# Linear attention and gated MLP in one kernel: the head's inverse roots on GpSimd, its normalizations on ScalarE

## Chip, cores and metric

The kernel runs on one core of one Trainium2 chip. The metric is the time of one execution on the device, in microseconds (us). The engines are TensorE (PE in the profile, PEld for its weight loads), VectorE (DVE), ScalarE (ACT), GpSimd (POOL) and SyncE (SP), which issues the DMAs.

## The reference

Two parts follow each other: attention without a softmax, with 64 product features, and a gated MLP whose gate mixes along the sequence. Batch 4, 4 heads, 1088 positions, head size 32, so d_model is 128; d_ff is 1024.

```python
phi(x) = outer(S1 @ x, S2 @ x)                     # 8 x 8 features
attn   = (phi(q) @ (phi(k)^T v)) / (phi(q) @ sum(phi(k)) + 1e-6)
h      = gelu_tanh(attn @ w_in)
u, v   = h[:512], h[512:]
v_n    = (v - mean(v)) / sqrt(var(v) + 1e-6) * g_ln
v_s    = w_sg @ v_n + b_sg                         # along the 1088 positions
out    = attn + (u * v_s) @ w_out
```

## The kernel before

The sequence is cut into nine tiles of 128 positions (the last one holds 64 real ones) and, where it is the moving axis, into three chunks of about 363. Products that need full precision take each operand as a high and a low part (fp32r) and three matmuls; the low part is the difference of the value and its rounded high part, one DVE subtraction each.

The **head** does batch 0 up to its first spatial product, while the weights come in. Its steps: `k1`, `kp`, `k2`, `kv` build the attention's sums; `q2`, `qa`, `qp` the features of q; `q3`, `xt`, `tr`, `x1`, `x2` the attention's output, transposed into a high part `x_h` (ACT) and a low part `x_l` (DVE), three tiles at a time; `v1` the gate half of h for one tile of positions (three matmuls into `pv`); `gelu` on ACT; `bn` its statistics on DVE (`mv`). Then, for three groups of three tiles (`GROUPS`), `v2` computes the inverse root of the variance of three tiles at once, in 12 DVE instructions of three elements per partition (a start value by integer shift, then two steps of Newton's kind), which end in `rs`, the inverse root, and `nm`, minus mean times `rs`. `v3` normalizes one tile of v in place: on ACT for the tiles in `VA` (4, 6 and 8), on DVE for the others. `z` is the spatial product of one tile with one chunk, as a plain fp32 product of two matmul records (27 of them). Beside this stand the splits of `w_in` in two halves (`wi1`, `wi0`, seven 512-element DVE steps and two for the low part each) and of `w_out` (`wo`), the high parts of w (`whi`, ACT) and its low parts (`wlo`, DVE, 1.3 us each). A low part `w_l[t]` is needed by the main loop and may start when tile t-1 has had its products.

The head's order isn't written out. Each step is given to `Steps.at` with its engine, its assumed length, what it comes after, the PSUM banks that it takes, an extra delay (`late`), and a `tail`. `Steps.order` then goes through the head as a list planner: it takes the step that can start first, unless one on the same engine that becomes ready before that step's end has a way to the end that is longer by 0.5; among equals the longer way goes first. Loads go in their given order on SP, each with an assumed time to landing of 2 us plus what its place in the bytes so far (`self.dma`, in KB) gives at an assumed rate. The engines then run their instructions in this order; a step that is planned before its input really lands makes its engine wait, with all that is queued behind.

The **main loop** does, per batch, the spatial product of the other three column blocks (and of all four for later batches), the gate, and the output product, with the next batch's attention and statistics spread between (`Side`, with due times in `FIRST` and `LATER`). Its instructions are ordered by the framework's scheduler, not by `Steps`. Its first matmuls are queued behind the head's last `z`.

Of the kernel before, what the change touches and what calls it, by code (L numbers as in the profile page):

```python
# [11 lines left out]
I32 = mybir.dt.int32  # L12
I64 = mybir.dt.int64
AF = mybir.ActivationFunctionType
ALU = mybir.AluOpType
# [3 lines left out]
P = 128  # L19
NT = 9  # L20
SP = NT * P
# [6 lines left out]
EPS = 1e-6  # L28
# [1 line left out]
EX = (2, 4, 7)  # L30
FL = 7
GROUPS = ((0, 3), (3, 3), (6, 3))
VA = (4, 6, 8)
WARM = 14


# [18 lines left out]
def f32(ap):  # L55
    return ap.bitcast(F32)
# [11 lines left out]
def tile_kernel(ctx: ExitStack, tc: tile.TileContext, qd, kd, vd, sd, wd, bd, wind, gd, woutd, identd, outd):  # L68
    nc = tc.nc
    mm = nc.tensor.matmul  # L70
    V, A, G = nc.vector, nc.scalar, nc.gpsimd
# [11 lines left out]
    def run(steps):  # L83
        for _ in steps or ():
            pass
# [38 lines left out]
    class Attention:  # L124
# [4 lines left out]
        def load_kv(self):  # L129
            self.k = self.pool([P, SP], "kld", f"k{self.b}")  # L130
            load(self.k, kd[self.b])
            for p in range(2):
                load(vx[:, p * (NT + 1) : p * (NT + 1) + NT], vd[self.b, :, p])
# [42 lines left out]
        def load_q(self, j):  # L176
            ci, p = divmod(j, 2)
            c0, cw = CH[ci]
            self.q[j] = q = self.pool([P, CW], "qld", f"q{self.b}_{j}")
            for r in range(2):  # L180
                load(q[64 * r : 64 * r + 64, :cw], qd[self.b, 64 * p : 64 * p + 64, c0 : c0 + cw])
# [262 lines left out]
    class Plan:  # L444
# [5 lines left out]
        def at(self, times, f, *args, name=None, after=()):  # L450

            if not isinstance(times, tuple):
                todo = [lambda: f(*args)]
                times = (times,)
            else:
                state = {}

                def step(i):
                    if i == 0:
                        state["g"] = f(*args)  # L460
                    if i + 1 < len(times):
                        next(state["g"])
                    else:
                        run(state["g"])

                todo = [lambda i=i: step(i) for i in range(len(times))]
            n = len(self.steps)
            for i, t in enumerate(times):
                if n + i < len(self.over):
                    t = self.over[n + i]  # L470
                self.steps.append([t, todo[i], [n + i - 1] if i else after])
            if name is not None:
                self.names[name] = n, len(times)
# [96 lines left out]
    class Head:  # L570
# [7 lines left out]

        def load(self, name, kb, f, after=(), queue="SP"):
            self.dma += kb  # L580
            self.s.at(name, queue, 0.47 if queue == "SP" else 0.1, f, after, late=2.0 + max(0.0, self.dma / 260 - 1.5))

        def split64(self, name, hi, lo, raw, n, whole, after, late):

            tl = {}

            def tile(x):
                if x not in tl:
                    tl[x] = self.stage([P, n], f"d{x}" if n > 16 else f"s{x}", name + x, F32 if x in "te" else I32)
                return tl[x]  # L590

            def word(i):
                return raw().bitcast(I32).rearrange("p (n two) -> p n two", two=2)[:, :, i]

            d = 0.08 + n / 950
            t, e, g, m = (lambda x=x: tile(x) for x in "tegm")
            ti, ei = lambda: t().bitcast(I32), lambda: e().bitcast(I32)
            ops = [

                lambda: V.tensor_scalar(ti(), word(1), 3, 0x3FFFFFFF, op0=ALU.logical_shift_left, op1=ALU.bitwise_and),  # L600
                lambda: V.scalar_tensor_tensor(ti(), word(1), -(1 << 30), ti(), op0=ALU.bitwise_and, op1=ALU.bitwise_or),

                lambda: V.tensor_scalar(m(), word(1), 0x7FFFFFFF, None, op0=ALU.bitwise_and),
                lambda: V.scalar_tensor_tensor(t(), m(), float(0x38100000), t(), op0=ALU.is_ge, op1=ALU.mult),

                lambda: V.tensor_scalar(ei(), word(0), 8, None, op0=ALU.logical_shift_right),
                lambda: V.tensor_scalar(g(), ti(), -(1 << 23), None, op0=ALU.bitwise_and),
                lambda: V.scalar_tensor_tensor(e(), ei(), 2.0**-44, f32(g()), op0=ALU.mult, op1=ALU.mult),
            ]
            last = after  # L610
            for i, f in enumerate(ops):
                self.s.at((name, i), "V", d, f, last, late=0.07)
                last = [(name, i)]
            if whole is not None:
                self.s.at((name, "whole"), "V", d, lambda: V.tensor_add(whole, t(), e()), last, late=0.07)
            more = [(name, "whole")] if whole is not None else []
            self.s.at((name, "hi"), "A", 0.1 + n / 1000, lambda: A.copy(hi, t()), [(name, 3)], late=0.08, tail=late)
            self.s.at(
                (name, "l1"), "V", d, lambda: V.tensor_sub(t(), t(), f32(hi)), [(name, "hi"), (name, 5)] + more, late=0.07
            )  # L620
            self.s.at((name, "l2"), "V", d, lambda: V.tensor_add(lo, t(), e()), [(name, "l1"), (name, 6)], late=0.07, tail=late)

        def build(self):
            at, pool, stage, g = self.s.at, self.pool, self.stage, self.g
# [130 lines left out]
            for c in range(3):  # L755
                at(("k1", c), "PE", 0.8, lambda c=c: k1(c), ["sk", "k0" if c == 0 else "k1"], [(("pk", c), "ps", 3)])
                at(("kb", c), "A", 0.2, lambda c=c: copy_b(c), [("k1", c)], late=0.1)
                for i in range(3):
                    t = 3 * c + i
# [21 lines left out]
            for j in range(6):  # L781
                c, p = divmod(j, 2)
# [7 lines left out]
            n = 2 * (D + 1)  # L790
            pd, px, den, xt = {}, {}, {}, {}
# [75 lines left out]
                at(("gelu", t), "A", 0.52, lambda t=t: gelu(t), [("v1", t)], (), [("pv", t)], late=0.1)  # L867
                at(("bn", t), "V", 0.8, lambda t=t: stats(t), [("gelu", t)], late=0.05)
            for t0, n_ in GROUPS:
                gen = g.v2(t0, n_)  # L870
                at(("v2", t0), "V", 1.8, lambda gen=gen: run(gen), [("bn", t) for t in range(t0, t0 + n_)], late=0.06)
                last = [("v2", t0)]
                for t in range(t0, t0 + n_):
                    if t in VA:
                        at(("v3", t), "A", 0.72, lambda t=t: g.v3(t), last, late=0.1)
                    else:
                        at(("v3", t), "V", 0.35, lambda t=t: V.tensor_scalar(  # L877
                            g.vn[:, t], g.vn[:, t], g.mv[:, t, 0:1], g.rs[:, t : t + 1], op0=ALU.subtract, op1=ALU.mult
                        ), last, late=0.08)
            zs = self.zs = []  # L880

            def z(t, ci):
# [26 lines left out]
            for i in range(3):  # L909
                gen = g.split(1, 3 * i, 3)  # L910
# [6 lines left out]
    def xtiles(b, xp):  # L917
        return [xp.tile([P, SP], F32R, name=f"x{b % 2}_{i}", tag=f"x{b % 2}_{i}") for i in "hl"]
# [3 lines left out]
    side = Pool(sp, 1, r=8, kp=3, kb=2, qld=1, qt=3, st=2, vh=2, vl=2, ve=3, y=3, h=3, p=3)  # L922

    x0 = xtiles(0, xp0)
    g = Gate(0, side, x0)
    with tc.tile_pool(name="stage", bufs=1) as stp:
        head = Head(side, Pool(stp, 1, wst=2, kb0=2, den=2, bst=2), x0, g)
        head.build()
        head.last = head.s.run(("z", NT - 1, 2), ("vl", 2), ("whi", NT - 1))
        zs = head.zs  # L930
    xp1 = ctx.enter_context(tc.tile_pool(name="x1", bufs=1, reuse_waits="tile"))
    gp = ctx.enter_context(tc.tile_pool(name="gate", bufs=2, reuse_waits="tile"))
    late = Pool(gp, 3, gt=4)
    pend = []

    def start():

        gts = [g.scale(late, zs[ci], 0, ci) for ci in range(3)]

        def unit(ci):  # L940
            pend.append(g.gate(late, gts[ci], g.unit(late, 0, ci), 0, ci))

        return [lambda ci=ci: unit(ci) for ci in range(3)] + 2 * [lambda: flush(late, *pend.pop(0))]
# [42 lines left out]
    for b in range(B):  # L986
        first, extra = (1, start()) if b == 0 else (0, [])
        if b + 1 < B:
# [7 lines left out]
            g = s.g  # L996
# [40 lines left out]
```

## Time and profile before

| | |
|---|---|
| median of three runs | 372.48 us (372.02 to 372.65) |
| the profiled execution | 372.73 us, span 370.9 us |
| PE busy | 356.7 us (96%) |
| DVE busy | 267.2 us (72%) |
| ACT busy | 160.0 us (43%) |
| POOL busy | 23.5 us (6%) |
| mean granted PE clock | 0.987 of 2.4 GHz |

The span reaches from the first to the last instruction; the device time also holds what lies around it. A busy share is a mean over stages that have different limits, so the stages are read one by one. In a row of a timeline the first two numbers are the start and the length in us; what stands in brackets is the idle time of the engine just before, and whose signal ended it. PEclk is the clock that TensorE was granted, as a part of 2.4 GHz.

### The profile page before, as it was taken

How to read it: one execution, taken by the hardware profiler on the slowest of the kernel's cores; microseconds unless marked ns; L12 is line 12 of the kernel's file. 1: busy time of each engine (PE TensorE's matmuls, PEld its weight loads, DVE VectorE, ACT ScalarE, POOL GpSimd, SP SyncE). 2: the span in 40 equal slices, each digit the busy share in tenths (PEclk: the TensorE clock that was granted, in tenths of full speed). 3: DMA queues.
4: the chain of work that ended last, by engine and by line, in shares of the span. 5: the costliest groups of instructions: out<-in, count | busy, mean ns of one | idle time of the engine just before them, and what ended most of it. 6: DMA issues, size and time to landing. Idle time of an engine off the chain costs nothing.

```text
span 370.9 us, 5565 instructions
## 1 busy us (share of the span) xinstructions
PE 356.7 (96%) x2067; PEld 331.5 (89%) x2067; DVE 267.2 (72%) x650; ACT 160.0 (43%) x349; POOL 23.5 (6%) x36
## 2 busy tenths in 40 slices
PE   8996899999999999999999999999999999999994
PEld 7883357899978999999989999999999999999993
DVE  5689999989699776699898555698888553633233
ACT  5268530155452872435534842334643941331120
POOL 4000000020220000202200000202200000000000
PEclk9998899999999999999999999999999999999998
DMA  7991000050110100411000000110000000100001
GB/s 245 411 394 71 0 3 0 23 163 5 45 37 14 29 0 13 157 44 59 23 20 2 0 0 2 42 40 21 2 0 2 0 1 22 40 2 0 2 0 60
DMA packets 9770, 18.46 MB, mean 50 GB/s; under 512 B 1680, under 2 KB 6672, under 8 KB 9744
## 3 DMA queue, kind: packets, MB, share of 16 engines
q1 hardware_dynamic: 9744, 18.11, 14.4%
q8 instruction: 16, 0.26, 0.3%
q14 instruction: 10, 0.08, 0.1%
HBM read 15.88 MB, written 2.23 MB: 49 GB/s over the span
## 4 chain that ended last, share of the span: by engine, by line
PE 64%; DVE 12%; ACT 2%; DMA 2%; issue 2%; SPq 0%; DVEq 0%
PE pz L334 13%; PE pz L333 13%; PE pz L332 13%; DMA q<-in_q 2%; PE pkv L158 2%; PE pu L346 2%; PE pu L347 2%; PE po L395 2%; PE pu L348 2%; PE po L396 2%; PE po L397 2%; PE pz L336 2%; PE pz L337 2%; PE pv L257 2%; PE pv L256 1%
## 5 line engine op out<-in xcount | busy, mean ns | idle before, releaser
L332 PE MATMUL pz<-w_h,vh 128*128 128x364 f32 (+1 forms) x360 | 119.6, 333 | 0.0
L334 PE MATMUL pz<-w_l,vh 128*128 128x364 f32 (+1 forms) x360 | 118.4, 329 | 0.3 <-DVE w_l L901 0.3
L333 PE MATMUL pz<-w_h,vl 128*128 128x364 f32 (+1 forms) x360 | 117.8, 327 | 0.0
L332 PEld LDWEIGHTS pz<-w_h,vh 128*128 128x128 f32 x360 | 67.7, 188 | 0.9 <-DVE gt L358 0.3
L333 PEld LDWEIGHTS pz<-w_h,vl 128*128 128x128 f32 x360 | 67.8, 188 | 0.6
L334 PEld LDWEIGHTS pz<-w_l,vh 128*128 128x128 f32 x360 | 67.6, 188 | 0.8 <-DVE w_l L901 0.6
L371 ACT CAST gh<-gt 128x362 fp32r<-128x362 f32 (+1 forms) x47 | 23.2, 495 | 86.4 <-PE po L396 80.6
L358 DVE SCALAR_TENSOR_TENSOR gt<-pz,g_col,b_bc 128x362 f32<-128x362 f32 (+1 forms) x48 | 28.0, 589 | 38.8 <-PE pz L337 38.3
L209 POOL TENSOR_TENSOR qpl<-qp,qph 128x362 fp32r<-128x362 f32 (+1 forms) x18 | 18.4, 1025 | 183.3 <-ACT kb L141 92.7
L372 DVE TENSOR_TENSOR gl<-gt,gh 128x362 fp32r<-128x362 f32 (+1 forms) x47 | 25.8, 551 | 5.1 <-ACT gh L371 4.9
L322 DVE TENSOR_TENSOR vl<-vn,vh 128x384 fp32r<-128x384 f32 (+2 forms) x60 | 22.9, 419 | 8.2 <-ACT vh L317 8.1
L351 ACT ACTIVATE u<-pu 128x362 f32<-128x362 f32 (+1 forms) x48 | 22.4, 471 | 12.3 <-PE pu L348 12.0
L304 ACT ACTIVATE vn<-vn,nm,rs 128x512 f32<-128x512 f32 x30 | 23.2, 810 | 9.8 <-DVE nm L299 9.8
L366 DVE TENSOR_TENSOR gt<-gt,u 128x362 f32<-128x362 f32 (+1 forms) x48 | 26.8, 560 | 0.4 <-ACT u L351 0.2
L317 ACT CAST vh<-vn 128x384 fp32r<-128x384 f32 (+1 forms) x63 | 23.4, 420 | 1.8 <-DVE vn L877 1.0
L228 DVE RECIPROCAL den<-den 128x362 f32<-128x362 f32 (+1 forms) x9 | 21.7, 2415 | 3.1 <-ACT den L225 2.9
L887 PE MATMUL pz<-w_f,vn 128*128 128x362 f32 (+3 forms) x54 | 20.0, 520 | 3.4 <-DVE vn L877 3.4
L887 PEld LDWEIGHTS pz<-w_f,vn 128*128 128x128 f32 (+1 forms) x54 | 10.5, 204 | 13.1 <-DVE vn L877 6.4
L261 ACT ACTIVATE vn<-pv 128x512 f32<-128x512 f32 x27 | 15.7, 595 | 12.5 <-PE pv L258 12.4
L264 DVE BATCH_NORM_STATS2 st<-vn 128x6 f32<-128x512 f32 x27 | 18.3, 686 | 3.6 <-ACT vn L261 3.5
L346 PE MATMUL pu<-x_h,win_h 128*128 128x362 f32 (+1 forms) x48 | 16.7, 348 | 1.1 <-DVE x L232 0.7
L347 PE MATMUL pu<-x_h,win_l 128*128 128x362 f32 (+1 forms) x48 | 15.7, 328 | 0.0
(166 smaller groups left out, 602.7 us busy)
## 6 DMA issues: line engine op xcount, KB each, us to landing
w_f<-in_w SPq DMA_DIRECT2D x9, 544.0 KB, 8.6
vx<-in_v SPq DMA_DIRECT2D x8, 288.0 KB, 4.1
q<-in_q SPq DMA_DIRECT2D x24, 90.5 KB, 2.5
k<-in_k SPq DMA_DIRECT2D x3, 576.0 KB, 3.9
out<-o SPq DMA_DIRECT2D x8, 181.0 KB, 1.9
q<-in_q SPq DMA_DIRECT2D x12, 91.0 KB, 2.5
win_raw<-in_w_in SPq DMA_DIRECT2D x2, 512.0 KB, 7.0
out<-o SPq DMA_DIRECT2D x4, 182.0 KB, 1.8
```

Source lines behind the costliest of these rows:

```text
L304: A.activation(self.vn[:, t], self.vn[:, t], AF.Identity, bias=self.nm[:, t : t + 1], scale=self.rs[:, t : t + 1])
L317: A.copy(vh[:, ts], vs[:, ts])
L332: mm(z, lhsT=vh[:, t], rhs=w_h[:, t, cs], start=(t == 0), stop=False)
L333: mm(z, lhsT=vl[:, t], rhs=w_h[:, t, cs], start=False, stop=False)
L334: mm(z, lhsT=vh[:, t], rhs=w_l[t][:, cs], start=False, stop=False)
L346: mm(pu, lhsT=win_h[:, ws], rhs=xh[:, cs], start=True, stop=False)
L347: mm(pu, lhsT=win_l[:, ws], rhs=xh[:, cs], start=False, stop=False)
L358: V.scalar_tensor_tensor(gt, z, g_col[:, db : db + 1], b_bc[:, c0 : c0 + cw], op0=ALU.mult, op1=ALU.add)
L366: V.tensor_mul(gt, gt, u)
L371: A.copy(gh, gt)
L372: V.tensor_sub(gl, gt, f32(gh))
L887: return mm(zs[ci], lhsT=g.vn[r, t, :P], rhs=w_f[t][r, c0 : c0 + cw], start=(t == 0), stop=(t == NT - 1),)
```

## The change

For the groups that begin at tiles 0 and 3 the 12-instruction chain `v2` is replaced by a new helper `norm`: its first three instructions stay on DVE, and the rest, twelve instructions with the two fused ones taken apart, go to GpSimd. The third group keeps its chain on DVE. All nine normalizations `v3` go to ACT; `VA` goes away. The planner is told a rate of 360 KB per us for the loads in place of 260, and the new lengths, and so draws up the order of all the head's steps anew. The small tiles of the chains get three buffers each in the head's pool.

```diff
@@ -30,7 +30,6 @@
 EX = (2, 4, 7)
 FL = 7
 GROUPS = ((0, 3), (3, 3), (6, 3))
-VA = (4, 6, 8)
 WARM = 14
 
 
@@ -578,7 +577,7 @@
 
         def load(self, name, kb, f, after=(), queue="SP"):
             self.dma += kb
-            self.s.at(name, queue, 0.47 if queue == "SP" else 0.1, f, after, late=2.0 + max(0.0, self.dma / 260 - 1.5))
+            self.s.at(name, queue, 0.47 if queue == "SP" else 0.1, f, after, late=2.0 + max(0.0, self.dma / 360 - 1.5))
 
         def split64(self, name, hi, lo, raw, n, whole, after, late):
 
@@ -620,6 +619,34 @@
             )
             self.s.at((name, "l2"), "V", d, lambda: V.tensor_add(lo, t(), e()), [(name, "l1"), (name, 6)], late=0.07, tail=late)
 
+        def norm(self, t0, n):
+
+            g, ts = self.g, slice(t0, t0 + n)
+            ve, y, h, p = (self.stage([P, n], "n" + x, f"n{x}0_{t0}") for x in "vyhp")
+            yi = y.bitcast(I32)
+
+            def first():
+                V.tensor_scalar(ve, g.mv[:, ts, 1], EPS, -0.5, op0=ALU.add, op1=ALU.mult)
+                V.tensor_scalar(yi, ve.bitcast(I32), 1, None, op0=ALU.logical_shift_right)
+                V.tensor_scalar(yi, yi, -1.0, float(0x9EF759DF), op0=ALU.mult, op1=ALU.add)
+
+            def rest():
+                G.tensor_mul(h, y, y)
+                G.tensor_mul(h, h, ve)
+                G.tensor_scalar(p, h, 1.5, 2.5, op0=ALU.mult, op1=ALU.add)
+                G.tensor_mul(p, p, h)
+                G.tensor_scalar(p, p, 1.875, None, op0=ALU.add)
+                G.tensor_mul(y, p, y)
+                G.tensor_mul(h, y, y)
+                G.tensor_mul(h, h, ve)
+                G.tensor_scalar(h, h, 1.5, None, op0=ALU.add)
+                G.tensor_mul(g.rs[:, ts], h, y)
+                G.tensor_scalar(p, g.mv[:, ts, 0], -1.0, None, op0=ALU.mult)
+                G.tensor_mul(g.nm[:, ts], p, g.rs[:, ts])
+
+            self.s.at(("first", t0), "V", 0.5, first, [("bn", t) for t in range(t0, t0 + n)], late=0.1)
+            self.s.at(("norm", t0), "G", 2.5, rest, [("first", t0)], late=0.1)
+
         def build(self):
             at, pool, stage, g = self.s.at, self.pool, self.stage, self.g
             sab_f = stage([P, 2, 2 * P], "sab_f", "sab_f")
@@ -867,16 +894,13 @@
                 at(("gelu", t), "A", 0.52, lambda t=t: gelu(t), [("v1", t)], (), [("pv", t)], late=0.1)
                 at(("bn", t), "V", 0.8, lambda t=t: stats(t), [("gelu", t)], late=0.05)
             for t0, n_ in GROUPS:
-                gen = g.v2(t0, n_)
-                at(("v2", t0), "V", 1.8, lambda gen=gen: run(gen), [("bn", t) for t in range(t0, t0 + n_)], late=0.06)
-                last = [("v2", t0)]
+                if t0 < 6:
+                    self.norm(t0, n_)
+                else:
+
+                    at(("norm", t0), "V", 1.9, lambda t0=t0, n_=n_: run(g.v2(t0, n_)), [("bn", t) for t in range(t0, t0 + n_)], late=0.06)
                 for t in range(t0, t0 + n_):
-                    if t in VA:
-                        at(("v3", t), "A", 0.72, lambda t=t: g.v3(t), last, late=0.1)
-                    else:
-                        at(("v3", t), "V", 0.35, lambda t=t: V.tensor_scalar(
-                            g.vn[:, t], g.vn[:, t], g.mv[:, t, 0:1], g.rs[:, t : t + 1], op0=ALU.subtract, op1=ALU.mult
-                        ), last, late=0.08)
+                    at(("v3", t), "A", 0.75, lambda t=t: g.v3(t), [("norm", t0)], late=0.1)
             zs = self.zs = []
 
             def z(t, ci):
@@ -924,7 +948,7 @@
     x0 = xtiles(0, xp0)
     g = Gate(0, side, x0)
     with tc.tile_pool(name="stage", bufs=1) as stp:
-        head = Head(side, Pool(stp, 1, wst=2, kb0=2, den=2, bst=2), x0, g)
+        head = Head(side, Pool(stp, 1, wst=2, kb0=2, den=2, bst=2, nv=3, ny=3, nh=3, np=3), x0, g)
         head.build()
         head.last = head.s.run(("z", NT - 1, 2), ("vl", 2), ("whi", NT - 1))
         zs = head.zs
```

## Rows read from the trace of the kernel before

**Rows 1.** Windows by stage: us from-to, length, busy us (instructions) per engine, PEclk, DMA share, GB/s.
```profile
core 0: us, PE busy (x) PEld busy (x) DVE busy (x) ACT busy (x) POOL busy (x), PEclk, DMA share, GB/s
20.00:30.00 10.00, 10.00 (x60) 7.92 (x58) 8.57 (x22) 6.51 (x12) 0.00 (x0) 1.00 0.98 366
40.00:45.00 5.00, 3.38 (x9) 1.54 (x9) 4.69 (x16) 3.62 (x5) 0.00 (x0) 0.94 0.00 0
80.00:370.00 290.00, 284.66 (x1696) 276.32 (x1695) 199.53 (x467) 125.31 (x279) 17.48 (x17) 1.00 0.08 24
```

**Rows 2.** PE's waits before 60 us: us in total, times, longest.
```profile
PE pz L887 <- DVE vn L877: 3.4, 4, 1.4
PE pv L855 <- DVE x_l L832: 2.1, 1, 2.1
```

**Rows 3.** Timeline of PE: start, us, instruction, [idle time before it].
```profile
22.65 1.55 PE L799 MATMUL pnd<-kvx,qp 128*128 128x66 f32 x12
...
24.68 0.48 PE L853 MATMUL pv<-win_h,x_h 128*128 128x512 f32 x1
...
25.45 0.40 PE L853 MATMUL pv<-win_h,x_h 128*128 128x512 f32 x1
...
32.82 0.50 PE L855 MATMUL pv<-win_h,x_l 128*128 128x512 f32 x1 [2.07 <-DVE x_l L832]
...
36.59 4.00 PE L887 MATMUL pz<-w_f,vn 128*128 128x364 f32 x6 [1.22 <-DVE vn L877]
...
47.01 11.82 PE L887 MATMUL pz<-w_f,vn 128*128 128x364 f32 x36 [0.61 <-DVE vn L877]
58.76 0.43 PE L346 MATMUL pu<-x_h,win_h 128*128 128x364 f32 x1
```

**Rows 4.** Window of PE's low clock: length, PE busy, PEclk, DMA share, GB/s.
```profile
33.80:40.62 6.82, 5.57 (x10) 0.50 0.00 0
```

**Rows 5.** Timeline of DVE: first and last of 12 chain instructions, and the next x_l.
```profile
29.61 0.17 DVE L276 TENSOR_SCALAR ve<-mv 128x3 f32<-128x3 f32 x1
...
31.80 0.16 DVE L299 SCALAR_TENSOR_TENSOR nm<-mv,rs 128x3 f32<-128x3 f32 x1
...
32.21 0.55 DVE L832 TENSOR_TENSOR x_l<-px,x_h 128x384 fp32r<-128x384 f32 x1
```

**Rows 6.** Normalizations: three in DVE's timeline; ACT's by line 304, head only (min/median/max ns).
```profile
46.41 1.45 DVE L877 TENSOR_SCALAR vn<-vn,mv,rs 128x512 f32<-128x512 f32 x3
...
L304 ACT ACTIVATE vn<-vn,nm,rs x3: 799/813/815, 38.9 to 46.7; 128x512 f32<-128x512 f32 x3
```

**Rows 7.** GpSimd's small instructions: a group before 60 us (busy us, mean ns), and line 691.
```profile
L1023 POOL MEMSET const-float32-0.0<- 128x1 f32 x1 | 0.1, 103 | 0.2 <-issue 0.2
...
L691 POOL TENSOR_SCALAR sab_h<-s_sp,mask x4: 437/441/446, 3.7 to 5.0; 128x64 fp32r<-128x64 f32 x4
```

**Rows 8.** GpSimd and DVE at 81 us, line 174 (ns), and a split step of w_in.
```profile
80.99 0.99 POOL L209 TENSOR_TENSOR qpl<-qp,qph 128x364 fp32r<-128x364 f32 x1 [3.05 <-ACT qph L207]
...
81.18 1.08 DVE L174 TENSOR_TENSOR kv_l<-kv,kv_h 128x256 fp32r<-128x256 f32 x1
...
L174 DVE TENSOR_TENSOR kv_l<-kv,kv_h x3: 417/425/1079, 81.2 to 242.6; 128x256 fp32r<-128x256 f32 x3
...
29.04 0.66 DVE L601 SCALAR_TENSOR_TENSOR wi0t<-win_raw,wi0t 128x512 int32<-128x512 int32 x1
```

**Rows 9.** DMA issues at 4.0 and in 12.4 to 14.5 us: KB each, us to landing; SP's timeline.
```profile
win_raw<-in_w_in SPq DMA_DIRECT2D x1, 512.0 KB, 6.2
...
w_f<-in_w SPq DMA_DIRECT2D x2, 544.0 KB, 11.5
...
10.71 3.61 SPq L649 DMA_DIRECT2D w_f<-in_w  x5
```

**Rows 10.** Timeline of PE where it waits for the last low parts of w.
```profile
64.10 0.43 PE L334 MATMUL pz<-w_l,vh 128*128 128x364 f32 x1 [0.31 <-DVE w_l L901]
...
65.72 0.41 PE L337 MATMUL pz<-w_l,vh 128*128 128x364 f32 x1 [0.35 <-DVE w_l L901]
```

**Rows 11.** Timelines of ACT and GpSimd at GpSimd's first TENSOR_TENSOR.
```profile
76.35 0.49 ACT L207 CAST qph<-qp 128x364 fp32r<-128x364 f32 x1
...
76.99 0.96 POOL L209 TENSOR_TENSOR qpl<-qp,qph 128x364 fp32r<-128x364 f32 x1 [11.70 <-ACT qph L207]
```

## The prediction

> **What bounds the kernel now.** I read the windows by stage first. From 20 to 30 us TensorE (PE) is busy all the time, and from 80 to 370 us for 284.66 of 290 us [rows 1]: what the head hands over late, the rest can't make up, and nearly every us by which PE leaves the head earlier is won. So the question is when PE leaves the head. The list of PE's waits before 60 us has, beside one at the very start, two entries: 3.4 us on the normalized v and 2.1 us on x_l [rows 2]. PE's timeline puts them in place. PE runs without a gap until v1 of tile 5 wants x_l, waits 2.07 us to 32.82, starts the first spatial product at 36.59 after another 1.22 us, waits for v three more times, and from 47.01 runs through to 58.76, where the main loop's first matmul stands [rows 3]. Its granted clock is 0.50 from 33.80 to 40.62 us, that is 1.2 GHz instead of 2.4; the fall comes about 1 us after the end of the 2.07 us wait [rows 4].
>
> Both kinds of wait end on VectorE (DVE), which is nearly full here: 4.69 of 5 us from 40 to 45 [rows 1]. The head's first inverse root is one chain of 12 instructions of three elements each, from 29.61 to 31.96, and the x_l that PE waits for stands right behind it on DVE, at 32.21 [rows 5].
>
> **The changes, part by part.**
>
> *Inverse roots to GpSimd.* Three instructions of a chain stay on DVE (a quarter of 2.35 us, 0.6), twelve go to GpSimd. For groups 0 and 3 DVE saves 2 x (2.35 - 0.6) = 3.5 us; group 6 stays as it was [rows 5].
>
> *Normalizations to ScalarE (ACT).* Six of nine leave DVE: three take 1.45 us, so six take 2.9. On ACT one takes 0.81 us, six more 4.9 [rows 6]. In its fullest stretch after 35 us ACT is busy for 3.62 of 5 us [rows 1], and PE wants one new tile only every 2 us (three products), so ACT can give them in time; what it delays is the casts of w, wanted much later. DVE saves 3.5 + 2.9 = 6.4 us in all.
>
> *The price of the GpSimd chain.* No row of before shows GpSimd arithmetic on three elements. From below: a MEMSET of one element, 0.10 us, so 12 x 0.10 = 1.2. From above: the TENSOR_SCALAR of 64 elements, 0.44, so 12 x 0.44 = 5.3 [rows 7]. The kind of work is that of the upper row, the size that of the lower; I take 0.30, nearer to the upper one because each instruction here waits for the one before, and 3.6 us for twelve.
>
> *What GpSimd and DVE do to each other.* While a GpSimd subtraction ran from 80.99 to 81.98, a DVE subtraction of two SBUF operands took 1.08 us, where its median is 0.425: it ended only after GpSimd's. DVE loses little to short GpSimd instructions, but w_in's split steps on DVE, 0.66 us with two SBUF operands, may hold the chain in turn; about three can fall into it, so 0 to 2 us [rows 8]. I take 0 for the sum, since such a step would have to start just ahead of a GpSimd instruction each time, and keep 2 us for a rival. The Trainium skill (SBUF — State Buffer, "Who interferes with whom") says that such a pair shuts each other out for the whole instruction and that whichever came first wins; the 1.08 us agree, and by it the sum below would come out near zero gain.
>
> *The order.* The shorter load times move steps in the order, not the transfers. The new due times stay behind the landings: the first half of w_in is issued at 4.01 and lands 6.2 us later, at 10.2, where the new plan has 9.8 plus the 0.7 us by which SP starts late; the last w_f lands near 25.4 (the last of five issues from 10.71 on, 11.5 us) against a plan of 32 [rows 9]. So no engine should come to stand before a load. Followed by hand, the planner's rule now puts the k products before most of the q products, w_in's second split partly before the statistics, and, because the way behind the first three v1 has grown longer, these ahead of the third q3 (1.45 us) and the third transpose. PE stays packed; the first three v1 come some 1.4 us before 24.68 [rows 3]. Their statistics then end near 27.5 rather than 29.1 us; the third xt (0.9 us) is put before the short DVE part, which ends near 29.1. The x_l of the last tiles follows near 33, so v1 of tiles 6 to 8 now stands on PE's queue **behind** the first two spatial products: where GpSimd is late, they are late too.
>
> *The sum.* Chain on GpSimd from 29.1 to 32.7; ACT 0.8 and two hand-overs 0.2: first spatial product at 33.7 instead of 36.59. PE runs out of other work near 31.0 (30.75 and the third matmul of tile 5), so it waits 2.7 us. Left from there: three v1 at 0.77 (24.68 to 25.45) and 27 spatial products at 0.657 (two records each, 36 in 11.82) [rows 3]: 2.3 + 17.7 = 20.0 us at full clock. The next groups are ready in time: group 3, behind the last gelus on ACT, at about 40, group 6 at about 45, when PE is at its fifth. A wait of 2.7 us is longer than the one ahead of the fall of the clock, so I take the same fall, 6.82 us at half the clock, a loss of 3.4 us [rows 4]; with no fall it would be 0. PE leaves the head at 33.7 + 20.0 + 3.4 = 57.1 us, 1.7 earlier than 58.76.
>
> Behind it stand the low parts of w: PE waited 0.31 and 0.35 us for the last two [rows 10]. DVE saves 6.4 us, less about 1.5 in which it would wait for the last gelus: 4.9 earlier, more than PE's 1.7, so these 0.7 us go as well. Gain 1.7 + 0.7 = 2.4 us. The profiled execution took 372.73 us (span 370.9), which gives 370.3; the median of the three runs is 0.25 lower, so I predict 370.1.
>
> **Rivals.**
> 1. *Clean head.* GpSimd needs 1.2 us; first spatial product at 31.3, where PE has just ended its other work; no fall of the clock. PE could leave at 51.3, but DVE's last w_l is only 6.4 us earlier, so the gain is DVE's, about 6: 366.5. For it: nothing else stands in the way of the first product. Against it: the 0.44 us row, and that any idle time of DVE comes off.
> 2. *The chain eats the gain.* 0.44 us each, 5.3 in all: product at 35.4, PE leaves at 35.4 + 20.0 + 3.4 = 58.8, no earlier than now. Only the 0.7 us on w_l are left: 371.8 to 372.5, no change that can be told.
> 3. *Slower: the chain stands in front of v1.* With 0.44 us each and the 2 us in which DVE's two-operand steps hold it, the chain takes 7.3; product at 37.4, v1 of tiles 6 to 8 behind it, PE leaves at 60.8; with the 0.7 saved that is 1.4 us slower, 373.9. It decides from a chain of 5.9 us (0.49 an instruction) on.
> 4. *A price for the first call.* GpSimd's first TENSOR_TENSOR moves into the head. In before it starts at 76.99, 0.15 us after the end of the ACT cast that it waits for (76.35 + 0.49) [rows 11], so a price of more than 0.15 us is not to be seen and the time would stay as forecast. The Trainium skill (GPSIMD Engine Reference, "2.1 Instruction dispatch") states about 6 us for the first call of a freshly loaded kernel; by it the kernel would come out near 376. The row speaks against that: 0.02, within rival 3's chance.
>
> About 1 us either way comes from the main loop: its order is drawn up by the framework, not written out, and in its first stretch it hangs on DVE, which leaves the head after PE.
>
> **How the numbers follow.** Forecast (gain 0.8 to 4.4): 0.50. Clean head: 0.20. Eaten gain: 0.17. Slower, rivals 3 and 4: 0.13. From about 0.2% (0.75 us) on a difference can be told from none; so faster is 0.70, same 0.17, slower 0.13. The range reaches from just below the clean head, 366.3, to 373.3, between rivals 2 and 3; about 0.05 is left out below and 0.1 above.
>
> **What would show it.** Right: twelve GpSimd instructions of about 0.3 us behind each short DVE part, the first spatial product at 33 to 34 us, PE idle for some 2.7 us before it and a stretch at half clock after it, no wait of PE on v between the groups, the main loop from about 57, no wait on w_l. Wrong: GpSimd instructions above 0.49 us; a wait of PE or ACT on a DMA in the first 25 us, which would mean that the order runs ahead of the loads; statistics of the last group so late that PE waits before tile 6; a shorter head with PE's waits after 60 us grown by as much.

## The result and the profile after

| | before | changed |
|---|---|---|
| median | 372.25 us (371.84 to 372.65, 4 runs) | 368.33 us (367.63 to 369.51, 4 runs) |
| profiled execution, span | 372.73 us, 370.9 us | 367.63 us, 365.9 us |

The ratio is 0.9898, 95% interval 0.987 to 0.9926: 3.9 us faster, where 2.4 were forecast. A second comparison on another chip gave 0.9892 (0.9878 to 0.9906).

From the page of the changed kernel: busy us (share of the span) and instructions of four engines, and the granted clock in 40 slices.

```profile
PE 353.1 (97%) x2067; PEld 331.1 (91%) x2067; DVE 261.8 (72%) x626; ACT 163.8 (45%) x355; POOL 29.4 (8%) x60
...
PEclk9998999999999999999999999999999999999999
```

DVE has 5.4 us and 24 instructions less, ACT 3.8 us more, GpSimd 5.9 us more. The windows by stage, in the columns of [rows 1]:

```profile
30.00:35.00 5.00, 1.42 (x3) 0.88 (x4) 4.00 (x12) 2.28 (x4) 4.01 (x14) 0.81 0.03 12
35.00:40.00 5.00, 5.00 (x18) 3.65 (x17) 2.69 (x7) 3.52 (x7) 1.03 (x6) 0.85 0.01 2
...
80.00:365.90 285.90, 279.94 (x1671) 271.72 (x1669) 195.99 (x461) 122.99 (x275) 16.42 (x16) 1.00 0.07 22
```

From 80 us on PE is as full as before. What is new is a hole: from 30 to 35 us PE works 1.42 of 5 us, and DVE only 2.69 of 5 in the next five. PE's timeline through the hole and out of the head answers [rows 3] and [rows 10]:

```profile
28.71 0.83 PE L852 MATMUL px<-ident,xt 128*128 128x128 f32 x6
33.59 1.58 PE L911 MATMUL pz<-w_f,vn 128*128 128x364 f32 x2 [4.05 <-ACT vn L303]
34.42 1.17 PE L880 MATMUL pv<-win_h,x_h 128*128 128x512 f32 x1
...
37.75 16.59 PE L911 MATMUL pz<-w_f,vn 128*128 128x362 f32 x52
54.27 0.44 PE L345 MATMUL pu<-x_h,win_h 128*128 128x364 f32 x1
...
60.12 0.43 PE L333 MATMUL pz<-w_l,vh 128*128 128x364 f32 x1 [0.72 <-DVE w_l L925]
...
61.73 0.41 PE L336 MATMUL pz<-w_l,vh 128*128 128x364 f32 x1 [0.34 <-DVE w_l L925]
```

One wait of 4.05 us stands in place of [rows 2]'s 5.5 us, then the spatial products run without a stop. PE enters the main loop at 54.27 instead of 58.76, 4.5 us earlier, but then waits 1.06 us for low parts of w, where it was 0.66 [rows 10]. The main loop's instructions stand in the same order in both kernels on every engine, so nothing is won or lost there by order: the last output product starts at 365.2 us before and 360.5 after, 4.7 earlier.

DVE's timeline shows why the low parts are no earlier than they are; the last row is the same instruction in the kernel before:

```profile
33.69 0.41 DVE L606 TENSOR_SCALAR wi0g<-wi0t 128x512 int32<-128x512 int32 x1
37.11 0.69 DVE L889 BATCH_NORM_STATS2 st<-vn 128x6 f32<-128x512 f32 x1 [3.01 <-ACT vn L885]
...
60.31 1.27 DVE L925 TENSOR_TENSOR w_l<-w_f,w_h 64x1088 fp32r<-64x1088 f32 x1
...
64.30 1.27 DVE L901 TENSOR_TENSOR w_l<-w_f,w_h 64x1088 fp32r<-64x1088 f32 x1
```

DVE stands idle for 3.01 us until the gelu of tile 6, and its last low part of w starts at 60.31, where it was 64.30: 4.0 us earlier. PE's 4.5 us shrink to the same 4.0 at its wait for a low part (60.12 against 64.10). The two profiled executions differ by 5.1 us, more than these 4.0: 0.7 us comes up bit by bit over the main loop and the rest in its last few us, and no single row stands for it.

GpSimd's timeline of the first chain, with the DVE instructions beside it:

```profile
28.65 0.19 POOL L634 TENSOR_TENSOR nh<-ny 128x3 f32<-128x3 f32 x1 [21.77 <-DVE ny L631]
28.92 0.19 POOL L635 TENSOR_TENSOR nh<-nh,nv 128x3 f32<-128x3 f32 x1
...
30.91 0.75 POOL L642 TENSOR_SCALAR nh<-nh 128x3 f32<-128x3 f32 x1
...
31.90 0.50 POOL L644 TENSOR_SCALAR np<-mv 128x3 f32<-128x3 f32 x1
32.49 0.19 POOL L645 TENSOR_TENSOR nm<-np,rs 128x3 f32<-128x3 f32 x1
...
30.88 0.66 DVE L600 SCALAR_TENSOR_TENSOR wi0t<-win_raw,wi0t 128x512 int32<-128x512 int32 x1
...
31.94 0.43 DVE L602 TENSOR_SCALAR wi0m<-win_raw 128x512 int32<-128x512 int32 x1
```

The twelve take 4.03 us (28.65 to 32.68). Most follow each other by 0.26 to 0.31 us, which would be some 3.4 in all; two take 0.75 and 0.50 us where the others take about 0.2, and each of the two runs beside a DVE split step.

### The profile page after: what moved, and what is told of

It is laid out like the page before. It is cut to its first block, busy times and chain, and to the rows that moved or that the text cites. A ratio compares the mean times of both kernels' runs of the same rounds, so it can differ in the third digit from the quotient of the medians.

```text
span 365.9 us, 5574 instructions
## 1 busy us (share of the span) xinstructions
PE 353.1 (97%) x2067; PEld 331.1 (91%) x2067; DVE 261.8 (72%) x626; ACT 163.8 (45%) x355; POOL 29.4 (8%) x60
## 3 DMA queue, kind: packets, MB, share of 16 engines
q1 hardware_dynamic: 9744, 18.11, 14.5%
## 4 chain that ended last, share of the span: by engine, by line
PE 67%; DVE 11%; ACT 2%; issue 2%; DMA 1%; SPq 0%; DVEq 0%
PE pz L331 14%; PE pz L333 14%; PE pz L332 14%; PE pkv L157 3%; PE pu L345 2%; PE pu L347 2%; PE pu L346 2%; PE po L394 2%; PE po L395 2%; PE po L396 2%; PE pz L336 2%; PE pz L335 2%; PE pv L256 2%; PE pv L257 1%; PE pv L255 1%
## 5 line engine op out<-in xcount | busy, mean ns | idle before, releaser
L333 PEld LDWEIGHTS pz<-w_l,vh 128*128 128x128 f32 x360 | 67.6, 188 | 1.2 <-DVE w_l L925 1.0
L303 ACT ACTIVATE vn<-vn,nm,rs 128x512 f32<-128x512 f32 x36 | 27.6, 809 | 10.0 <-DVE nm L298 7.3
L911 PE MATMUL pz<-w_f,vn 128*128 128x362 f32 (+3 forms) x54 | 18.2, 489 | 4.0 <-ACT vn L303 4.0
L347 PE MATMUL pu<-x_l,win_h 128*128 128x362 f32 (+1 forms) x48 | 15.8, 329 | 0.0
```

Source lines behind the costliest of these rows:

```text
L303: A.activation(self.vn[:, t], self.vn[:, t], AF.Identity, bias=self.nm[:, t : t + 1], scale=self.rs[:, t : t + 1])
L333: mm(z, lhsT=vh[:, t], rhs=w_l[t][:, cs], start=False, stop=False)
L347: mm(pu, lhsT=win_h[:, ws], rhs=xl[:, cs], start=False, stop=True)
L911: return mm(zs[ci], lhsT=g.vn[r, t, :P], rhs=w_f[t][r, c0 : c0 + cw], start=(t == 0), stop=(t == NT - 1),)
```

## The experiments

The theory after this reading: what ends the head is DVE's last low part of w, and the gain is the DVE time set free, less the 3.01 us that DVE waits. That wait goes back to one place: v1 of tiles 6 to 8 stands on PE's queue behind a spatial product that waits for GpSimd and ACT. The rivals: the gain is the new order that the load rate gives; PE, with its wait and its low clock, is the bound and not DVE.

**1. The new load rate alone, on the kernel before.**

```diff
-  late=2.0 + max(0.0, self.dma / 260 - 1.5)
+  late=2.0 + max(0.0, self.dma / 360 - 1.5)
```

> The kernel before with the rate of 360 KB per us alone: a new order, no work moved off VectorE. Theory (the gain is VectorE's freed time, passed on through the last low parts of w): VectorE's work is the same, only a gap or two before 25 us is filled, so 0 to 1 us faster, 371.2 to 372.3. Rival (the gain is the new order): 3 us or more faster, below 369.3.

372.2 us, ratio 0.9987 (0.9972 to 1.0001). The order alone is worth 1 us at most.

**2. The two chains on GpSimd alone, on the kernel before.**

```diff
-  at(("v2", t0), "V", 1.8, ...)
+  self.norm(t0, n_)          # groups 0 and 3
```

> The kernel before with the two chains on GpSimd alone (normalizations and load rate as before). Theory: VectorE saves 3.5 us, of which the wait for the last gelus may take back up to 2: 1.5 to 3.5 us faster, 368.8 to 370.8. Rival (new order): within 1 us of before.

366.86 us, ratio 0.9856 (0.9837 to 0.9874): 5.6 us faster than before, and 1.5 better than the whole change. The theory's range was too cautious, and the reason is in this kernel's order: with normalizations on DVE the planner puts v1 of all tiles ahead of the first spatial product, PE waits for x_h and x_l before it (0.57 and 1.88 us), and DVE never stands idle for a gelu. What it does not save on the normalizations it does not lose by waiting. Run 4 differs from this one by the place of the normalizations and the order that follows from it, and is 1.4 us slower on the same chip: with the chains on GpSimd, and in the order that the planner then draws up, moving the normalizations to ACT costs time. The first chain took 3.75 us, and PE's first product came as late as 35.78:

```profile
32.70 0.19 POOL L646 TENSOR_TENSOR nm<-np,rs 128x3 f32<-128x3 f32 x1
...
35.78 2.41 PE L917 MATMUL pz<-w_f,vn 128*128 128x364 f32 x6
...
59.00 1.27 DVE L931 TENSOR_TENSOR w_l<-w_f,w_h 64x1088 fp32r<-64x1088 f32 x1
```

An early first product is worth nothing by itself: the last low part of w comes at 59.00 here, 1.3 us before the changed kernel's, and the median is 1.5 us lower.

**3. All normalizations on ACT alone, on the kernel before.**

```diff
-  if t in VA: ... "A" ...  else: ... "V" ...
+  at(("v3", t), "A", 0.75, lambda t=t: g.v3(t), last, late=0.1)
```

> The kernel before with all normalizations on ScalarE alone (chains and load rate as before). Theory: VectorE saves 2.9 us, mostly behind the place where PE waits: 1.5 to 3 us faster, 369.3 to 370.8. Rival (new order): within 1 us of before.

369.85 us, ratio 0.9936 (0.9912 to 0.996): 2.7 us faster, as the DVE time set free says.

**4. The changed kernel with the old rate.** The edit is that of the first one turned round.

> The changed kernel with the old load rate of 260 KB per us. Theory: it keeps most of the gain, 3 to 4 us faster than before, 368.3 to 369.3. Rival (new order): it loses most of it, above 371.

368.27 us, ratio 0.9888 (0.9869 to 0.9906), as the changed kernel. With the first run this settles it: the new load times are not what the gain comes from.

**5. The changed kernel with all inverse roots on DVE.**

```diff
-  if t0 < 6: self.norm(t0, n_)
-  else: at(("norm", t0), "V", ...)
+  at(("norm", t0), "V", ...)
```

> The changed kernel with all three inverse roots on VectorE again (new rate and ScalarE's normalizations kept). Theory: VectorE has 3.5 us more to do, ahead of the x_l that v1 waits for, but the first product no longer waits for GpSimd: 1 to 3 us slower than the changed kernel, 369.3 to 371.3. Rival (the chain on GpSimd is a loss that the rest makes up): faster than the changed kernel, below 368.

369.63 us, ratio 0.9932 (0.9919 to 0.9945): 1.3 us slower than the changed kernel. PE where it enters the main loop and where it waits there, DVE's last low part, and the window of PE's low clock (length, PE busy, PEclk, DMA share, GB/s):

```profile
53.24 0.43 PE L345 MATMUL pu<-x_h,win_h 128*128 128x364 f32 x1
...
59.37 0.43 PE L332 MATMUL pz<-w_h,vl 128*128 128x364 f32 x1 [1.12 <-DVE vl L321]
...
61.01 0.67 PE L333 MATMUL pz<-w_l,vh 128*128 128x364 f32 x1 [0.71 <-DVE w_l L922]
...
61.21 1.27 DVE L922 TENSOR_TENSOR w_l<-w_f,w_h 64x1088 fp32r<-64x1088 f32 x1
...
60.90:64.30 3.40, 3.29 (x12) 0.50 0.00 0
```

With the chains on DVE the planner puts all v1 ahead of the first spatial product again, and DVE waits for no gelu longer than 0.23 us. So the chains cost DVE 3.5 us here, but the wait of 3.0 us for the gelu is gone, and the last low part starts at 61.21 instead of 60.31 (61.24 in run 11, a second profile of the changed kernel). PE enters the main loop 1.0 us before the changed kernel's and wins nothing by it: it waits for DVE, and behind these waits its clock falls once more.

**6. Four more instructions in each GpSimd chain.**

```diff
+  for _ in range(4):
+      G.tensor_scalar(h, h, 1.0, None, op0=ALU.mult)
   G.tensor_scalar(p, g.mv[:, ts, 0], -1.0, None, op0=ALU.mult)
```

> The changed kernel with four more instructions in each of GpSimd's two chains (the same element times 1.0 on a tile that is no longer needed): 4 x 0.28 = 1.1 us later. Theory: the chain stands ahead of the first product, v1 of tiles 6 to 8, their statistics and so VectorE's last low part of w, so all of it shows: 1.1 us slower than the changed kernel, 369.4. Rival (PE's wait for the low parts of w, 1.0 us in all, covers it): no change, 368.3.

370.28 us, ratio 0.9943 (0.9926 to 0.996): 1.9 us slower than the changed kernel, more than the 1.1 forecast. GpSimd's added four in the first chain, and DVE's wait:

```profile
31.66 2.15 POOL L645 TENSOR_SCALAR nh<-nh 128x3 f32<-128x3 f32 x4
...
38.71 0.70 DVE L891 BATCH_NORM_STATS2 st<-vn 128x6 f32<-128x512 f32 x1 [4.98 <-ACT vn L887]
```

The four take 2.15 us there, beside DVE's split steps, and the first chain 5.99 instead of 4.03. PE waits 5.92 us, DVE 4.98 instead of 3.01 for the gelu of tile 6, and DVE's last low part starts at 61.89, 1.6 us later (0.65 later than in run 11). PE's slack does not cover it: the chain stands in the line that ends at DVE's last w_l. The half clock lasts 6.8 us, as in run 11.

**7. Matmuls of no use in PE's wait.** They go into a free PSUM bank behind the third transpose.

```diff
+  if n == ("tr", 2):
+      for _ in range(16): mm(o[:64, :64], lhsT=mask, rhs=mask, start=True, stop=True)
```

> The changed kernel with 16 small matmuls of no use (64 x 64 of the mask into a free bank) put behind the third transpose, into PE's wait for the first normalized tile. Theory: the clock does not fall, so the first product and v1 of tile 6 are about 1.4 us shorter, the last gelus and VectorE's work behind them as much earlier: 1 to 1.5 us faster than the changed kernel, 366.8 to 367.3. Rival (the fall of the clock has nothing to do with the wait, or VectorE is not late for that reason): no change, 368.3.

366.65 us, ratio 0.9847 (0.9832 to 0.9862): 1.7 us faster than the changed kernel. The window of PE's low clock in the changed kernel (length, PE busy, PEclk, DMA share, GB/s), then PE and DVE here:

```profile
33.00:36.43 3.43, 2.85 (x6) 0.51 0.00 0
```

```profile
29.76 2.08 PE L859 MATMUL fill<-mask 128*64 128x64 f32 x32
33.78 0.88 PE L919 MATMUL pz<-w_f,vn 128*128 128x364 f32 x2 [1.94 <-ACT vn L303]
34.22 0.67 PE L888 MATMUL pv<-win_h,x_h 128*128 128x512 f32 x1
...
36.02 0.69 DVE L897 BATCH_NORM_STATS2 st<-vn 128x6 f32<-128x512 f32 x1 [1.72 <-ACT vn L893]
```

The granted clock is 1.0 until the last few us of the execution. The first product takes 0.88 us instead of 1.58, and the same chain of v1, gelu and statistics lets DVE go on at 36.02 instead of 37.11. Over all five executions the mean granted clock is 0.995 to 1.0, against 0.991 to 0.995 in the changed kernel's. So the fall of the clock comes with the wait, and it hurts through DVE: PE itself enters the main loop 1.16 us earlier (53.11) and waits for w_l as long as in the changed kernel (0.71 and 0.35).

**8. x_l and v1 ahead.** The planner's list is edited before it is run.

```diff
+  late_v1 = [("v1", 6), ("v1", 7), ("v1", 8), ("gelu", 6), ("gelu", 7)]
+  # move ("x2", 2) ahead of ("bn", 5), and late_v1 ahead of ("v3", 0)
```

> The changed kernel with the last x_l put ahead of the statistics of tile 5 on VectorE, v1 of tiles 6 to 8 ahead of the first spatial product on PE, and the gelus of tiles 6 and 7 ahead of the first normalization on ScalarE. Theory: v1 fills PE's 4.05 us wait, VectorE's 3.0 us wait for the gelu of tile 6 goes, and its last low part of w comes about 3 us earlier: 2 to 3 us faster than the changed kernel, 365.3 to 366.3. Rival (the wait is only moved, to the first product's own path or to w_l): within 0.7 us of the changed kernel.

365.31 us, ratio 0.9819 (0.9799 to 0.9838): 3.0 us faster than the changed kernel, 6.9 than before.

```profile
34.11 17.31 PE L918 MATMUL pz<-w_f,vn 128*128 128x364 f32 x54 [0.69 <-ACT vn L303]
51.35 0.44 PE L345 MATMUL pu<-x_h,win_h 128*128 128x364 f32 x1
...
56.15 0.43 PE L332 MATMUL pz<-w_h,vl 128*128 128x364 f32 x1 [0.42 <-DVE vl L321]
57.79 0.43 PE L333 MATMUL pz<-w_l,vh 128*128 128x364 f32 x1 [0.71 <-DVE w_l L932]
59.41 0.40 PE L336 MATMUL pz<-w_l,vh 128*128 128x364 f32 x1 [0.35 <-DVE w_l L932]
```

PE's 4.05 us wait is down to 0.69, the clock does not fall, and PE is in the main loop at 51.35; it waits there 1.48 us for DVE. The theory holds, and PE still waits for DVE.

**9. The third chain on GpSimd too, on top of 8.** DVE's order is kept.

```diff
-  else: at(("norm", t0), "V", 1.9, lambda: run(g.v2(t0, n_)), ...)
+  else: at(("norm", t0), "V", 1.9, lambda: (first(), rest()), ...)
```

> The version with x_l and v1 ahead, and with the third inverse root on GpSimd as well, all else in the same order. Theory (VectorE's last low part of w sets the end of the head): VectorE saves 1.7 us more; PE waits 1.5 us for low parts there now, so up to 1.5 us faster than that version, 363.8 to 364.6. Rival (PE is the bound by now, or the third chain holds the last normalizations up): no change or slower, 365.3 or more.

368.24 us, ratio 0.9892 (0.9873 to 0.9911): 2.9 us **slower** than 8. The theory fails, and the second half of the rival holds: the third chain holds the last normalizations up. The timelines of GpSimd, ACT and DVE:

```profile
41.30 0.96 POOL L645 TENSOR_SCALAR np<-np 128x3 f32<-128x3 f32 x1
42.34 1.13 POOL L646 TENSOR_TENSOR ny<-np,ny 128x3 f32<-128x3 f32 x1
...
45.70 2.22 ACT L303 ACTIVATE vn<-vn,nm,rs 128x512 f32<-128x512 f32 x3 [4.37 <-POOL nm L652]
...
42.13 1.29 DVE L931 TENSOR_TENSOR w_l<-w_f,w_h 128x1088 fp32r<-128x1088 f32 x1
...
49.47 0.69 DVE L625 TENSOR_TENSOR wot<-wot,wout_h 128x512 f32<-128x512 f32 x1 [4.64 <-ACT wout_h L623]
```

Here DVE is in its long run of split steps and low parts, and the same twelve instructions take 6.55 us (39.12 to 45.67) instead of the 3.53 of this run's first chain. The first nine each end 0.04 to 0.09 us behind the end of a DVE instruction, as if they waited for it; the last three, beside which DVE stands idle, take 0.20 to 0.23 us. Then the queue does the rest: ACT stands 4.37 us before the normalizations, the cast of w_out stands behind them, and DVE waits 4.64 us for that cast. The Trainium skill (SBUF — State Buffer, "Who interferes with whom") says that the two engines exclude each other for a whole instruction when DVE reads two SBUF operands or runs in a two-port mode; the 1.13 us of a three-element instruction beside a 1.29 us subtraction agree.

**10. PE's order alone: the first two products behind v1, on the changed kernel.**

```diff
+  # move ("z", 0, 0), ("z", 0, 1) behind ("v1", 8)
```

> The changed kernel with the first two spatial products put behind v1 of tiles 6 to 8 on PE, and nothing else. Theory: the gelu of tile 6 comes right behind the three normalizations on ScalarE, at about 35.0 instead of 36.5 us, VectorE's wait of 3.0 us shrinks by 1.5: 1 to 1.5 us faster than the changed kernel. Rival (the place of x_l on VectorE is what counts, not PE's order): within 0.5 us of it.

366.72 us, ratio 0.9842 (0.9827 to 0.9857), 1.7 us faster than the changed kernel on the same chip (368.4). DVE's wait:

```profile
36.15 0.69 DVE L896 BATCH_NORM_STATS2 st<-vn 128x6 f32<-128x512 f32 x1 [1.35 <-ACT vn L892]
```

1.35 us instead of 3.01. The clock still falls, for 3.4 us from 34.6 on, behind PE's wait of 1.96 us for x_l that ends at 33.58.

**11. The changed kernel once more.**

> The changed kernel once more, for a comparison on the same chip: 1.0 to 1.1% faster than before, 368.3.

368.4 us, ratio 0.9892 (0.9878 to 0.9906). In this second profile of the changed kernel the window of PE's low clock, PE's entry into the main loop and DVE's last low part are

```profile
32.68:39.52 6.84, 5.75 (x12) 0.51 0.00 0
...
55.82 0.44 PE L345 MATMUL pu<-x_h,win_h 128*128 128x364 f32 x1
...
61.24 1.27 DVE L925 TENSOR_TENSOR w_l<-w_f,w_h 64x1088 fp32r<-64x1088 f32 x1
```

The first chain (4.04 us), PE's wait (4.06) and DVE's (3.01) are those of the first profile, but the half clock lasts 6.8 us and not 3.4. PE enters the main loop 1.55 us later, DVE waits 0.37 us more for each of the next two gelus, and the last low part starts 0.9 us later; this execution took 368.46 us, the first 367.63. So the length of the fall is not fixed by the kernel, and a difference of some 1 us between the heads of two single profiles can be this alone.

**12. The split of w_out behind the low parts of w, on top of 8.**

```diff
+  wo = [n for n in names if isinstance(n, tuple) and n[0] == "wo"]
+  # move wo behind ("wlo", 8)
```

> The version with x_l and v1 ahead, and with the split of w_out (eight VectorE steps and a cast) put behind the last low part of w, where it stood ahead of the second one. Theory (VectorE's last low part of w sets the end of the head): it comes some 4 to 5 us earlier, the 1.48 us that PE waits for VectorE there go, and PE is the bound: 1.5 us faster than that version, 363.8, unless the split comes late for the first output products. Rival (what VectorE has to do in all before 70 us is what counts, not where the low parts stand in it): no change, 365.3.

363.6 us, ratio 0.9772 (0.9752 to 0.9793): 1.7 us faster than 8 and 8.8 than before.

```profile
50.85 0.44 PE L345 MATMUL pu<-x_h,win_h 128*128 128x364 f32 x1
...
53.49 1.27 DVE L936 TENSOR_TENSOR w_l<-w_f,w_h 64x1088 fp32r<-64x1088 f32 x1
```

The last low part starts 4.5 us earlier than in 8, PE no longer waits for any, and no more is won than PE's own terms: the 1.5 us that it had waited and the 0.5 by which it enters the main loop earlier; the profiled executions differ by 2.1 us (363.6 and 365.67). So PE is the bound from here. That is read from this sum and not tested by itself: in this run the framework also orders the main loop anew, where the other runs keep its order but for a few instructions at its start.

The runs side by side, all times from the one profiled execution of each, in us. The last column is the length of the execution less the start of the last low part of w:

| kernel | PE enters main loop | last low part starts | execution | difference |
|---|---|---|---|---|
| before | 58.76 | 64.30 | 372.73 | 308.4 |
| 1, rate alone | 58.04 | 62.83 | 370.57 | 307.7 |
| 6, longer chain | 55.95 | 61.89 | 369.74 | 307.9 |
| 3, ACT alone | 52.98 | 61.33 | 370.89 | 309.6 |
| 11, changed again | 55.82 | 61.24 | 368.46 | 307.2 |
| 5, no GpSimd | 53.24 | 61.21 | 369.65 | 308.4 |
| 9, third chain | 53.45 | 60.79 | 368.98 | 308.2 |
| 4, old rate | 54.86 | 60.35 | 368.36 | 308.0 |
| changed | 54.27 | 60.31 | 367.63 | 307.3 |
| 10, v1 ahead | 54.08 | 59.33 | 367.17 | 307.8 |
| 7, filled wait | 53.11 | 59.23 | 366.56 | 307.3 |
| 2, GpSimd alone | 54.78 | 59.00 | 367.08 | 308.1 |
| 8, x_l and v1 ahead | 51.35 | 57.99 | 365.67 | 307.7 |
| 12, w_out late | 50.85 | 53.49 | 363.60 | 310.1 |

In twelve of the fourteen the end follows that one DVE instruction at 307.2 to 308.4 us. PE's entry into the main loop does not order them: run 3 enters 5.8 us before the kernel before and ends 1.8 us before it, run 5 enters 5.5 us before it and ends 3.1. This answers the second rival. Run 3 lies 1.2 us outside the band: its granted clock is 0.50 a second time, from 60.8 to 67.6 us, behind PE's waits for DVE. In runs 5 and 9 such a second stretch lasts 3.4 us, and they stand near the band's upper end. Run 12 leaves the line because PE no longer waits for a low part. The low part is a mark of how far DVE's queue has come: in runs 2 and 4 PE waits not for it but for `kp`, which stands beside it on DVE.

## Why the prediction was right

The direction came out and the size lay within the range, 2.4 forecast and 3.9 us measured; but the engine that set the size was not the one that the sum went by. By its steps:

- *What bounds.* "Nearly every us by which PE leaves the head earlier is won" is the sentence that does not hold: in run 3 PE left 5.8 us earlier for a gain of 2.7. Only what DVE gives back is won, as long as PE waits for DVE in the main loop.
- *DVE's savings.* 6.4 us forecast; the busy time, which leaves out the gaps between the tiny instructions, fell by 5.4. The wait for the last gelus was put at 1.5 us and was 3.01. DVE's gain was thus forecast at 4.9 us; with the wait as it was, the same sum gives 3.4. The last low part came 4.0 us earlier in one profile and 3.1 in the other.
- *The GpSimd chain.* 0.30 an instruction and 3.6 us were taken; it was about 0.28 where nothing ran against it, and 4.03 in all. The 0.30 was a choice between 0.10 and 0.44, so that it came so near is in part luck. Of the 0 to 2 us that DVE's steps might add 0.6 came true.
- *The order.* As followed by hand: v1 of tiles 0 to 2 ahead of the third q3, x_l of the last tiles at 32.29, v1 of tiles 6 to 8 behind the first spatial product, one and not two.
- *The first product.* 33.7 forecast, 33.59 measured, and this too is luck in part: the chain began at 28.65 and not 29.1 and took 4.03 us and not 3.6, two errors of 0.4 us that cancel. PE's wait before it was 4.05 and not 2.7, since PE had run out of other work at 29.5 and not at 31.0.
- *The clock.* The same fall as in the kernel before, 6.82 us, was taken. It came in run 11 (6.8 us) and not in the first profile (3.4). PE left the head at 55.82 and 54.27, against 57.1. From its first product on it took 22.05 and 20.68 us, where 27 products at 0.638 and three v1 at 0.70 make 19.3 at full clock: the clock cost 2.7 and 1.4 us and not 3.4, since the fall has already begun when the first product starts. Another 0.5 us is the products' price, 0.638 us each (52 records in 16.59) against 0.657.
- *The last step.* The sum gave PE 2.4 us (1.7, and 0.7 of waits that would vanish) and DVE 4.9, and took the smaller gain. This form was right, but PE came 4.5 and 2.9 us earlier and DVE 4.0 and 3.1, so the waits did not vanish: they were 1.06 and 0.53 us. In the first profile the gain is DVE's, in the second the two are about equal. Two of the signs that were named for "right" thus failed: no wait on w_l, and the main loop from about 57.
- *The rivals.* The eaten gain did not come, because the chain took 4.0 us and not 5.3. Rival 3 is tested by run 6: its first chain took 5.99 us, above the 5.9 from which that rival makes the kernel slower than before, and it was still 1.9 us faster than before. The price of a first call did not show: GpSimd's first product starts 0.09 us behind the end of DVE's short part. The clean head is close to run 8, 6.9 us; the way to it was the order on PE, DVE and ACT, not a shorter chain.

## What to carry to other kernels

When two engines leave a stage, find which one the next stage meets last, and price a change on that engine alone; here the start of one DVE instruction gave the length of twelve executions within a band of 1.2 us, while PE's entry into the same stage did not. Gains of two moves need not add up: the chains alone gave 5.6 us, the normalizations alone 2.7, and both together 4.2 on the same chip (run 4). Work that is moved to a slower engine should not be waited for at the head of a queue that has other ready work: three matmul groups put ahead of the waiting one gave 1.7 us, and with their input ahead as well 3.0. A low-priority split that stands before the work that ends the stage is part of the bound, however late its result is needed: putting it behind gave another 1.7.

## What the runs showed of the hardware

A GpSimd instruction on three elements per partition costs 0.26 to 0.31 us from start to start, against 0.20 on DVE [rows 5], so a chain of tiny dependent steps is not far from DVE's own pace. What makes it dear here is what DVE runs beside it: the quickest chain took 3.53 us (the first one of run 9, one of its twelve longer), 4.03 with two beside split steps, 6.55 beside a run of split steps and low parts.

PE's clock fell to 1.2 GHz behind waits. Behind the same wait of about 4 us the fall lasted 3.4 us in one execution of the changed kernel and 6.8 in another; it was 6.8 us behind 5.9 us in run 6 and behind 2.07 us in the kernel before, and 3.4 behind 1.96 us in run 10. With matmuls of no use in the wait PE stayed at 2.4 GHz in the profile of run 7.
